# Attention and two expert layers on one core: VectorE, ScalarE and POOL put in a fixed order, as a pipeline in half steps

## The chip, the core and the metric

The kernel runs on one core of a Trainium2 chip. The metric is the time of one execution in microseconds (us). The core's engines are TensorE (PE in the rows; PEld is its weight load), VectorE (DVE), ScalarE (ACT), GpSimd (POOL) and SyncE (SP), which issues nearly all DMAs. TensorE's clock has two levels, 1.2 and 2.4 GHz; "granted clock" is the share of full speed.

## The reference

```python
kv  = einsum('bhsd,bhse->bhde', k, v)        # 4 batches, 8 heads, 576 rows, 64 wide
o   = einsum('bhsd,bhde->bhse', q, kv)
x   = o / rms(o) * g_norm                     # 2304 tokens x 512
h   = x @ w_in                                # 512 -> 2048, float64 weights
x   = where(h > 0, h, exp(min(h, 0)) - 1) @ w_out
for e in range(4):                            # w1[e]: 512 -> 1024, w2[e]: 1024 -> 512
    out += p[:, e:e+1] * (maximum(x @ w1[e], 0) @ w2[e])
```

## The kernel before

Every operand of a product is held as two parts, a rounded high part (ScalarE's copy) and the low remainder (a subtraction on POOL or VectorE, `split`), and a product is three matmuls: high x high, high x low, low x high. Tokens are worked on in 6 blocks j of 384.

*Attention and group zero* come from a table of places (`at_place`) and are emitted in that order with dependences that pin all four compute engines. *Layer one* then runs the other 14 columns c of 128 of the hidden layer in groups 1 to 4 (2, 4, 4 and 4 columns), each over all 6 blocks: a step (g, j, c) is `product1` (12 matmuls into a bank of 384 columns, two banks in turn), the ELU (`begin_elu`: two ScalarE operations; `end_elu`: one VectorE operation, line 465, which is the last to read the bank), `split_h`, and two steps later `emit_mm2` (12 matmuls). At a group's last column four accumulations (`into_acc`, line 483) go to VectorE. Beside this, `convert` turns the float64 rows of the next group's weights into float32 (five VectorE operations each, lines 151 to 179, two on ScalarE, then a split), 8 rows per group. `make_w` makes *forms*: layer two multiplies 2 x 2 blocks of each expert's weights with seven products P1 to P7 instead of eight, so that for each of 16 *quarters* (expert, w1 or w2, half) 7 combinations are made (4 subtractions on VectorE, line 232; a copy on ScalarE; a low part on POOL, or for two of the seven on VectorE once group four runs, line 241), stored to DRAM (`keptw`) and loaded again as `ws` when needed. `make_forms` makes the same combinations of the activations, once per pair of token blocks.

*Layer two* has 12 moves (3 pairs of token blocks x 4 experts). A move has 14 units of the first product (q, banks qa and qb) and, one move later, 14 of the second (m, banks ma and mb), which alternate. A unit is 12 matmuls, with its weights streamed four units ahead from DRAM by SP. P2 and P6 accumulate into the bank of P1 and P5, after ScalarE has copied that product out (lines 576, 655).

Behind the table of places nothing pins an engine's order: `emit_mm1`, `emit_mm2`, one step of `make_w` and so on are emitted one after another, and Tile's scheduler sets each engine's order by its own model of time:

```python
    for hh in range(2 * (len(steps) + LAG)):
        s, second = divmod(hh, 2)
        if not second and s < len(steps):
            emit_mm1(*steps[s][1:], nc.vector if s >= len(steps) - 3 else nc.gpsimd)
        if second and s >= LAG:
            emit_mm2(*steps[s - LAG])
        for op, *args in todo.get(hh, ()):
            op(*args)
```

## Time and profile before

| | us |
|---|---|
| median of 3 runs (lowest to highest) | 1253.01 (1250.71 to 1257.75) |
| the profiled execution | 1254.61 |
| its span in the trace | 1252.82 |
| PE, DVE, ACT, POOL busy | 1191.7, 794.6, 590.4, 664.2 |
| mean granted clock of TensorE | 0.977 |

The span goes from the first to the last instruction in the trace; the 1.8 us beside it lie outside. Busy times are shares of the whole span and mix stages with different limits. "Idle before" in a row is the engine's idle time just before the instruction, with what ended it.

### The profile page before, as it was taken

What the parts mean: (1) busy time and instruction counts of PE and PEld (TensorE: products, weight loads), DVE (VectorE), ACT (ScalarE), POOL (GpSimd) and SP (SyncE); (2) the same over time, 40 slices, a digit from 0 to 9 for tenths busy, and PEclk for the clock granted to TensorE, in tenths of its full rate; (3) what the DMA queues carried; (4) which work ended last, traced back from release to release, by engine and by line L of the source; (5) the groups of instructions that cost most, each with busy time, mean ns of one, the idle gap of its engine ahead of it and who ended that gap; (6) DMA issues with size and microseconds to landing.
All of it is one profiled execution on the core that took longest, in us unless ns stands there. A gap on an engine that the chain in (4) does not pass through costs nothing.

```text
span 1252.8 us, 18931 instructions
## 1 busy us (share of the span) xinstructions
PE 1191.7 (95%) x7039; PEld 1170.3 (93%) x7039; DVE 794.6 (63%) x950; ACT 590.4 (47%) x937; POOL 664.2 (53%) x521
## 2 busy tenths in 40 slices
PE   8899988897998999899999989999999899999997
PEld 8799978897998999899999989999999899999996
DVE  5878898969766456453546773546468545555475
ACT  3677665655555555443333434343345334333432
POOL 1124487688576568534455664445457634555533
PEclk9999988998998999999999999999999899999999
DMA  9943268666988765887887868878787688788883
GB/s 338 346 157 118 85 212 327 234 252 225 281 296 291 286 235 205 289 277 252 265 258 264 253 220 255 284 260 265 251 267 251 214 259 288 251 270 254 260 248 127
DMA packets 103455, 312.22 MB, mean 249 GB/s; under 512 B 19068, under 2 KB 23748, under 8 KB 101828
## 3 DMA queue, kind: packets, MB, share of 16 engines
q1 hardware_dynamic: 98532, 306.30, 73.2%
q10 hardware_dynamic: 4832, 4.72, 1.1%
q8 instruction: 56, 0.92, 0.3%
q14 instruction: 35, 0.29, 0.1%
HBM read 238.06 MB, written 72.91 MB: 248 GB/s over the span
## 4 chain that ended last, share of the span: by engine, by line
PE 52%; DVE 17%; DMA 8%; issue 5%; POOL 3%; ACT 2%; SPq 1%; POOLq 0%; DVEq 0%; ACTq 0%
PE ps_qb L552 15%; PE ps_mb L552 12%; PE ps_ma L552 11%; PE ps_qa L552 10%; DMA keptw<-wform 4%; DMA wraw<-in_moe_w_dram 3%; DVE wform L232 3%; POOL wform L241 1%; DVE acc L483 1%; DVE m L154 1%; DVE m L650 1%; DVE s L301 1%; DVE e L465 1%; DVE x L176 1%; DVE acc L651 1%
## 5 line engine op out<-in xcount | busy, mean ns | idle before, releaser
L193 POOL TENSOR_TENSOR h<-h 128x384 fp32r<-128x384 f32 x232 | 272.8, 1198 | 293.8 <-ACT h L183 292.4
L552 PE MATMUL ps_qb<-f,ws 128*128 128x384 f32 x1152 | 219.7, 338 | 9.1 <-DVE u L579 8.0
L183 ACT CAST h<-h 128x768 fp32r<-128x768 f32 x168 | 140.0, 835 | 164.7 <-PE ps_mb L552 83.1
L552 PEld LDWEIGHTS ps_qb<-f,ws 128*128 128x128 f32 x1152 | 203.6, 190 | 10.1 <-DVE u L579 8.6
L552 PE MATMUL ps_mb<-h,ws 128*128 128x384 f32 x1032 | 190.9, 335 | 0.7 <-ACT p L655 0.7
L552 PE MATMUL ps_ma<-h,ws 128*128 128x384 f32 x984 | 183.1, 334 | 2.0 <-ACT o L700 1.7
L552 PEld LDWEIGHTS ps_mb<-h,ws 128*128 128x128 f32 x1032 | 180.8, 189 | 1.3 <-ACT p L655 1.0
L552 PEld LDWEIGHTS ps_ma<-h,ws 128*128 128x128 f32 x984 | 171.5, 188 | 2.9 <-ACT o L700 1.9
L193 POOL TENSOR_TENSOR h<-e,h 128x384 fp32r<-128x384 f32 x91 | 107.1, 1179 | 114.5 <-ACT h L183 100.1
L552 PE MATMUL ps_qa<-f,ws 128*128 128x384 f32 x864 | 164.6, 335 | 1.3 <-DVE acc L483 1.3
L451 PE MATMUL ps_h<-x,w 128*128 128x384 f32 x384 | 135.6, 353 | 22.9 <-DVE e L465 22.9
L552 PEld LDWEIGHTS ps_qa<-f,ws 128*128 128x128 f32 x864 | 150.7, 188 | 1.8 <-DVE acc L483 1.8
L490 PE MATMUL ps_y<-h,w 128*128 128x384 f32 x384 | 131.7, 343 | 2.7 <-POOL h L193 2.7
L452 PE MATMUL ps_h<-x,w 128*128 128x384 f32 x384 | 132.6, 345 | 0.4 <-DVE x L427 0.4
L453 PE MATMUL ps_h<-x,w 128*128 128x384 f32 x384 | 132.6, 345 | 0.0
L491 PE MATMUL ps_y<-h,w 128*128 128x384 f32 x384 | 131.4, 342 | 0.1
L489 PE MATMUL ps_y<-h,w 128*128 128x384 f32 x384 | 117.9, 342 | 8.4 <-DVE acc L483 5.7
L572 ACT ACTIVATE h<-h 128x768 f32<-128x768 f32 x72 | 60.8, 847 | 119.6 <-DVE h L584 70.6
L451 PEld LDWEIGHTS ps_h<-x,w 128*128 128x128 f32 x384 | 75.3, 196 | 28.8 <-DVE e L465 28.6
L241 POOL TENSOR_TENSOR wform<-wform 128x512 fp32r<-128x512 f32 x54 | 77.0, 1430 | 31.9 <-ACT wform L239 11.8
L489 PEld LDWEIGHTS ps_y<-h,w 128*128 128x128 f32 x384 | 72.0, 191 | 11.8 <-DVE acc L483 7.8
L193 DVE TENSOR_TENSOR h<-h 128x768 fp32r<-128x768 f32 x52 | 50.5, 972 | 49.6 <-ACT h L183 49.6
(115 smaller groups left out, 1833.3 us busy)
## 6 DMA issues: line engine op xcount, KB each, us to landing
ws<-keptw SPq DMA_DIRECT2D x336, 512.0 KB, 4.4
keptw<-wform SPq DMA_DIRECT2D x112, 512.0 KB, 3.7
wraw<-in_moe_w_dram SPq DMA_DIRECT2D x32, 512.0 KB, 6.8
keptx<-x SPq DMA_DIRECT2D x6, 1536.0 KB, 6.0
x<-keptx SPq DMA_DIRECT2D x6, 1536.0 KB, 8.3
raw<-in_moe_w_in_dram SPq DMA_DIRECT2D x16, 512.0 KB, 4.4
raw<-in_moe_w_out_dram SPq DMA_DIRECT2D x16, 512.0 KB, 4.2
qkv<-in_k_dram SPq DMA_DIRECT2D x18, 256.0 KB, 5.4
```

The costliest lines, as they stand in the source:

```text
L183: nc.scalar.copy(hi, src)
L193: eng.tensor_tensor(out=l, in0=x, in1=h, op=ALU.subtract)
L232: nc.vector.tensor_tensor(out=f[:, 1], in0=minus[0], in1=minus[1], op=ALU.subtract)
L241: eng.tensor_tensor(out=f[:, 1].bitcast(F32R), in0=src, in1=f[:, 0], op=ALU.subtract)
L451: nc.tensor.matmul(ps, ah, bh, start=(kk == 0), stop=False)
L452: nc.tensor.matmul(ps, ah, bl, start=False, stop=False)
L453: nc.tensor.matmul(ps, al, bh, start=False, stop=(kk == KD - 1))
L489: nc.tensor.matmul(ps, bh[:, cols], hi, start=first, stop=False)
L490: nc.tensor.matmul(ps, bh[:, cols], lo, start=False, stop=False)
L491: nc.tensor.matmul(ps, bl[:, cols], hi, start=False, stop=last)
L552: nc.tensor.matmul(ps[:, c, :T], a, x[:, b, kk, :], start=start and kk == 0 and n == 0, stop=stop and kk == 1 and n == 2, skip_group_check ...
L572: nc.scalar.activation(into, src, AF.Relu)
```

## The change

Three things. First, behind the table of places VectorE, ScalarE and POOL now execute in the order in which the program emits (`in_program_order` at the end); TensorE and SP are still left to the scheduler. Second, the program emits in half steps (12 matmuls each). What follows from an operation on another engine is not emitted with it but put into a queue for a later half step (`after(n, ...)`, done by `tick`): an ELU's split comes one half step after its ending, a conversion's five operations are spread over five half steps, a form's low part comes one half step after its copy and its store another one later. In layer two a product is read out of its bank at the start of the next unit, ahead of all else. Third, the forms have tables of offsets: in layer one 12 of the 16 quarters are made, from group two on, 6 at 16 half steps each and 6 at 7; the last four are made in layer two's first pass over the experts, at 28 half steps each. A quarter's weights are loaded in four blocks of 256 KB ahead of time into six buffers, instead of two DMAs into one buffer. Before, the program's text also left some of the forms to layer two, but the scheduler did not: in the trace the first of the 64 subtractions on line 232 starts at 166.8 us and the last at 526.0 us, where layer two begins.

```diff
+    def after(n, op, *args):
+        queue.setdefault(clock[0] + n, []).append((op, args))
+
+    def tick(*starts):
+        for op, args in queue.pop(clock[0], []):
+            op(*args)
+        for op, *args in starts:
+            op(*args)
+        clock[0] += 1
...
+    def load_block(n, name):
...
+        b = blocks[n, name] = next_in("b", [P, 2, HK], "wraw")
+        row = (e * NC2 + half * NH + 2 * s) * P
+        nc.sync.dma_start(
+            out=b, in_=(w1, w2)[ab][row:row + 2 * P, cols * HK:(cols + 1) * HK].rearrange("(c p) f -> p c f", p=P)
+        )
...
+        def finish(name, of):
+            f = t[of] if of in t else next_in("f", [P, 2, 2, HK], "wform")
+            src = f[:, 1] if of in t else blocks[n, of]
             nc.scalar.copy(f[:, 0].bitcast(F32R), src)
+            after(1, finish_low, name, f, src)
+
+        def finish_low(name, f, src):
             eng = nc.vector if name in late["on_vector"] else nc.gpsimd
             eng.tensor_tensor(out=f[:, 1].bitcast(F32R), in0=src, in1=f[:, 0], op=ALU.subtract)
...
+            after(1, keep, name, f)
...
+    FORMS_SLOW = "t1:0 t2:2 P5:3 t3:4 t4:6 P3:7 b12:8 b11:8 P4:9 P7:10 b22:10 P1:11 P2:13 b21:14 P6:15", 16
+    FORMS_FAST = "t1:0 t2:1 P5:2 t3:2 b12:3 b11:3 b22:3 t4:3 P3:4 P4:4 P7:5 P1:5 P2:6 P6:7 b21:8", 7
+    FORMS_LATE = "t1:0 t2:4 P5:5 t4:8 P3:9 t3:12 P7:13 b12:14 P4:16 P1:18 P2:20 P6:22 b11:22 b22:25 b21:25", 28
...
         form("A11", a11, nc.gpsimd)
+        yield
         form("S2", s2, other)
         yield
         form("A12", a12, nc.gpsimd)
+        s4 = sums(a12, s2, ALU.subtract, s2)
+        yield
         form("S1", s1, other)
-        s4 = sums(a12, s2, ALU.subtract, s2)
+        yield
+        form("S4", s4, nc.gpsimd)
         s3 = sums(a11, a21, ALU.subtract, s1)
...
-    begins = 2 * (len(steps) - NB * NF)
...
-            for hh in range(begins, begins + length, every):
-                at_step(hh, make_one, converting)
-            at_step(begins + length - 1, finish_all, converting)
+            for n, row in enumerate(pieces):
+                at_step(begins + n * (3 if g == 1 else 6), convert, len(rows))
+                rows.append(row)
...
-            emit_mm1(*steps[s][1:], nc.vector if s >= len(steps) - 3 else nc.gpsimd)
-        if second and s >= LAG:
-            emit_mm2(*steps[s - LAG])
-        for op, *args in todo.get(hh, ()):
-            op(*args)
...
+        if not second:
+            if s < len(steps):
+                product1(*steps[s][1:])
+            while pending:
+                into_acc(*pending.pop(0))
+            if 0 < s <= len(steps):
+                split_h(*steps[s - 1][1:], nc.vector if s >= len(steps) - 2 else nc.gpsimd)
+            tick(*todo.get(hh, ()))
+        else:
+            if s >= LAG:
+                emit_mm2(*steps[s - LAG])
+            if s < len(steps):
+                begin_elu(*steps[s][1:])
+            tick(*todo.get(hh, ()))
+            if s < len(steps):
+                end_elu(*steps[s][1:])
...
+    for n in range(IN_LAYER1, len(quarters)):
+        at = plan_forms(n, at, FORMS_LATE, lambda half, step: starts.setdefault(half, []).append(step))
...
+            for kind in "qm":
+                if evict:
+                    evict()
+                evict = None
+                if kind == "q" and n < len(moves):
+                    stream(u + AHEAD)
+                    evict = emit_q(u, moves[n], *Q_UNITS[k])
+                    u += 1
...
+                tick(*starts.pop(clock[0], ()))
...
+    in_program_order(start_order, E_.DVE, E_.Activation, E_.Pool)
```

How the change moves instructions, at three places. The first is VectorE early in group two of layer one, before:

```order
L232 TENSOR_TENSOR wform<-wraw 128x512
L232 TENSOR_TENSOR wform<-wraw,wform 128x512 x2
L465 SCALAR_TENSOR_TENSOR e<-e,ps_h 128x384
L151 TENSOR_SCALAR x<-raw 128x512
L154 TENSOR_SCALAR m<-raw 128x512
L168 SCALAR_TENSOR_TENSOR m<-raw,m 128x512
L154 TENSOR_SCALAR m<-raw 128x512
L168 SCALAR_TENSOR_TENSOR m<-raw,m 128x512
L176 SCALAR_TENSOR_TENSOR x<-raw,x 128x512
L465 SCALAR_TENSOR_TENSOR e<-e,ps_h 128x384
```

and VectorE early in the same group now (lines 495, 507 and 261 are what 465, 483 and 232 were; 936 to 959 are four of the conversion's five operations):

```order
L495 SCALAR_TENSOR_TENSOR e<-e,ps_h 128x384
L507 TENSOR_TENSOR acc<-ps_y,acc 128x384 x4
L168 SCALAR_TENSOR_TENSOR m<-raw,m 128x512
L953 SCALAR_TENSOR_TENSOR x<-raw,x 128x512
L261 TENSOR_TENSOR wform<-wraw 128x512
L959 SCALAR_TENSOR_TENSOR m<-m,x 128x512
L495 SCALAR_TENSOR_TENSOR e<-e,ps_h 128x384
L261 TENSOR_TENSOR wform<-wraw,wform 128x512
L495 SCALAR_TENSOR_TENSOR e<-e,ps_h 128x384
L936 TENSOR_SCALAR x<-raw 128x512
```

Before, six conversion operations stood between two ELU endings, in runs that the scheduler chose. Now at most four operations stand there (two conversion operations and a subtraction among them).

The second is VectorE at the end of the first pair of token blocks in layer two, between the reading of the pair's last product (line 594, now 620) and that of the next pair's second one (579, now 604). Before:

```order
L594 TENSOR_TENSOR h<-ps_qb,u 128x768
L675 TENSOR_TENSOR c<-ps_ma,u 128x768
L650 TENSOR_TENSOR m<-c,p 128x768
L651 TENSOR_TENSOR acc<-acc,m 128x768
L599 TENSOR_TENSOR h<-h 128x768
L600 TENSOR_TENSOR h<-h 128x768
L601 TENSOR_TENSOR h<-h 128x768
L193 TENSOR_TENSOR h<-h 128x768
L579 TENSOR_TENSOR u<-ps_qb,p 128x768
```

and now:

```order
L620 TENSOR_TENSOR h<-ps_qb,u 128x768
L685 TENSOR_TENSOR acc<-acc,m 128x768
L327 TENSOR_TENSOR s<-acc 128x768
L713 TENSOR_TENSOR c<-ps_ma,u 128x768
L628 TENSOR_TENSOR h<-h 128x768
L684 TENSOR_TENSOR m<-c,p 128x768
L629 TENSOR_TENSOR h<-h 128x768
L685 TENSOR_TENSOR acc<-acc,m 128x768
L191 TENSOR_TENSOR f<-s,f 128x768
L604 TENSOR_TENSOR u<-ps_qb,p 128x768
```

Between the two readings stood seven operations; now there are eight, among them a sum and a low part of the new pair's forms (lines 327 and 191).

The third is SP, where layer two begins (`ws` is a weight tile that is loaded, `keptw` a form that is stored). Before, the last stores and then 40 loads in a row:

```order
L530 DMA ws<-keptw 128x1024
L247 DMA keptw<-wform 128x1024 x2
L530 DMA ws<-keptw 128x1024 x2
L247 DMA keptw<-wform 128x1024
L530 DMA ws<-keptw 128x1024 x40
L618 DMA p<-p_dram 128x768
L530 DMA ws<-keptw 128x1024 x27
```

and now, some way into the first pass:

```order
L555 DMA ws<-keptw 128x1024 x8
L276 DMA keptw<-wform 128x1024
L555 DMA ws<-keptw 128x1024 x5
L276 DMA keptw<-wform 128x1024
L555 DMA ws<-keptw 128x1024
L248 DMA wraw<-in_moe_w_dram 128x2x256
L555 DMA ws<-keptw 128x1024 x2
L276 DMA keptw<-wform 128x1024
L555 DMA ws<-keptw 128x1024 x2
```

Stores that wait for POOL or VectorE, and loads of blocks, now stand among the weight tiles through the whole first pass.

## Rows read from the trace of the kernel before

**Rows 1.** The page, parts 1 and 2: busy time, and clock in 40 slices.

```profile
PE 1191.7 (95%) x7039; PEld 1170.3 (93%) x7039; DVE 794.6 (63%) x950; ACT 590.4 (47%) x937; POOL 664.2 (53%) x521
...
PEclk9999988998998999999999999999999899999999
```

**Rows 2.** Waits of TensorE: who, for whom: us in total, times, longest.

```profile
PE ps_h L451 <- DVE e L465: 22.9, 14, 4.9
PE ps_qb L552 <- DVE u L579: 8.0, 2, 4.0
...
PE ps_y L489 <- ACT h L183: 1.9, 1, 1.9
...
PE ps_mb L552 <- ACT p L655: 0.7, 1, 0.7
```

**Rows 3.** Timeline of PE in group two: start us, us, instruction.

```profile
198.49 0.33 PE L451 MATMUL ps_h<-x,w 128*128 128x384 f32 x1
...
200.57 0.33 PE L489 MATMUL ps_y<-h,w 128*128 128x384 f32 x1
```

**Rows 4.** Stretches: us, busy of PE, PEld, DVE, ACT, POOL, clock, DMA share, GB/s.

```profile
106.60:159.60 53.00, 52.24 (x299) 51.36 (x298) 46.14 (x74) 36.00 (x70) 26.70 (x21) 1.00 0.31 93
159.60:285.30 125.70, 109.42 (x569) 106.33 (x569) 108.08 (x129) 74.60 (x143) 95.14 (x71) 0.92 0.71 258
285.30:408.60 123.30, 110.92 (x587) 106.84 (x586) 89.36 (x110) 66.34 (x131) 84.24 (x64) 0.93 0.83 275
408.60:510.00 101.40, 99.52 (x572) 98.66 (x571) 57.73 (x77) 54.47 (x105) 66.97 (x55) 1.00 0.70 246
```

**Rows 5.** The same view: around the end of TensorE's longest wait.

```profile
208.90:215.70 6.80, 4.65 (x15) 4.65 (x16) 5.03 (x7) 3.86 (x7) 4.56 (x4) 0.50 0.96 351
```

**Rows 6.** Timeline of VectorE in group two, the same columns as rows 3.

```profile
169.87 0.54 DVE L465 SCALAR_TENSOR_TENSOR e<-e,ps_h 128x384 f32<-128x384 f32 x1
...
171.29 1.76 DVE L232 TENSOR_TENSOR wform<-wraw,wform 128x512 f32<-128x512 f32 x1
172.98 0.68 DVE L168 SCALAR_TENSOR_TENSOR m<-raw,m 128x512 f32<-128x512 uint32 x1
...
178.10 0.54 DVE L465 SCALAR_TENSOR_TENSOR e<-e,ps_h 128x384 f32<-128x384 f32 x1
```

**Rows 7.** Groups by line, VectorE, group three: count | busy us, mean ns | idle before.

```profile
L232 DVE TENSOR_TENSOR wform<-wraw 128x512 f32<-128x512 f32 x12 | 14.7, 1227 | 10.9 <-DMA wraw<-in_moe_w_dram 9.1 <-issue 1.9
...
L232 DVE TENSOR_TENSOR wform<-wraw,wform 128x512 f32<-128x512 f32 x12 | 13.6, 1131 | 1.5 <-DMA wraw<-in_moe_w_dram 1.4
```

**Rows 8.** The page, part 6: DMA issues, KB each, us to landing.

```profile
ws<-keptw SPq DMA_DIRECT2D x336, 512.0 KB, 4.4
keptw<-wform SPq DMA_DIRECT2D x112, 512.0 KB, 3.7
wraw<-in_moe_w_dram SPq DMA_DIRECT2D x32, 512.0 KB, 6.8
...
x<-keptx SPq DMA_DIRECT2D x6, 1536.0 KB, 8.3
```

**Rows 9.** The same view as rows 4: the highest rates of transfer.

```profile
0.00:40.00 40.00, 36.00 (x409) 32.67 (x410) 23.90 (x51) 17.28 (x29) 3.51 (x11) 1.00 0.97 350
330.00:335.00 5.00, 5.00 (x30) 4.85 (x30) 4.47 (x5) 1.82 (x4) 3.96 (x3) 1.00 1.00 398
```

**Rows 10.** The same view, layer two: a steady stretch, two ends of pairs.

```profile
560.00:720.00 160.00, 160.00 (x925) 160.00 (x925) 90.67 (x88) 65.24 (x81) 82.68 (x66) 1.00 0.81 258
720.00:760.00 40.00, 36.00 (x200) 35.65 (x200) 26.31 (x22) 16.41 (x21) 28.57 (x21) 0.96 0.68 226
960.00:1000.00 40.00, 36.00 (x197) 35.65 (x197) 27.51 (x24) 15.06 (x19) 28.09 (x20) 0.91 0.65 219
```

**Rows 11.** Timeline of VectorE at the first end of a pair.

```profile
727.53 0.94 DVE L594 TENSOR_TENSOR h<-ps_qb,u 128x768 f32<-128x768 f32 x1
...
739.62 0.94 DVE L579 TENSOR_TENSOR u<-ps_qb,p 128x768 f32<-128x768 f32 x1
```

More of the change, by code (lines that the diff above doesn't have):

```diff
@@ L193, in split @@
             eng.tensor_tensor(out=l, in0=x, in1=h, op=ALU.subtract)
+    def split(hi, lo, src, eng):
+        nc.scalar.copy(hi, src)
+        split_lo(lo, src, hi, eng)
+    queue = {}
+    clock = [0]
+    def after(n, op, *args):
[6 more added lines that the diff above has]
+        clock[0] += 1
     wf = {}
@@ L212, in attention_moe_kernel @@
     kept_w = {}
[L214 to L238 removed]
+    IN_LAYER1 = 12
@@ new lines, in attention_moe_kernel, with next_in @@
+    quarters = [(ab, e, s) for e in range(E) for ab in (0, 1) for s in (0, 1)]
+    blocks = {}
+    rings = {"b": 0, "f": 0}
+    def next_in(ring, shape, name):
+        of = late[ring]
+        pool, tag = of[rings[ring] % len(of)]
+        rings[ring] += 1
+        return pool.tile(shape, F32, tag=tag, name=name)
+    def load_block(n, name):
+        if n >= len(quarters):
+            return
+        ab, e, s = quarters[n]
+        half, cols = (int(name[2]) - 1, int(name[1]) - 1) if ab == 0 else (int(name[1]) - 1, int(name[2]) - 1)
+        b = blocks[n, name] = next_in("b", [P, 2, HK], "wraw")
[3 more added lines that the diff above has]
+        )
@@ L239, in finish, with make_w, sum_ @@
+    def make_w(n):
+        ab, e, s = quarters[n]
+        t = {}
+        def sum_(name, a, b):
+            f = t[name] = next_in("f", [P, 2, 2, HK], "wform")
+            a, b = (t[x][:, 1] if x in t else blocks[n, x] for x in (a, b))
+            nc.vector.tensor_tensor(out=f[:, 1], in0=a, in1=b, op=ALU.subtract)
+        def finish(name, of):
+            f = t[of] if of in t else next_in("f", [P, 2, 2, HK], "wform")
+            src = f[:, 1] if of in t else blocks[n, of]
             nc.scalar.copy(f[:, 0].bitcast(F32R), src)
+            after(1, finish_low, name, f, src)
+        def finish_low(name, f, src):
@@ L323, in make_forms @@
         form("A22", a22, nc.gpsimd)
+        yield
     at = ExitStack()
@@ L752, in plan_norm, with in_program_order @@
             at_place(x, emit_x, t)
+    before = {}
+    E_ = mybir.EngineType
+    def in_program_order(begin, *engines):
+        for i in nc.cur_bb.bb.instructions[begin:]:
+            if i.engine not in engines:
+                continue
+            if i.engine in before:
+                tc.add_manual_dep(
+                    i, before[i.engine].name,
+                    mybir.DependencyInfo(mybir.DependencyClass.NoSync, mybir.DependencyReason.DATA),
+                    reason="order",
+                )
+            before[i.engine] = i
     def busy(n):
@@ L937, in attention_moe_kernel @@
         at_step(begins + hh, make_one, of_p)
-    of_forms = [begins + n for n in (22, 25, 28, 32, 36)]
-    for hh in of_forms:
-        at_step(hh, make_one, forms_of_0)
-    for hh in range(25, 2 * len(steps) - 4):
-        if hh == begins:
-            at_step(hh, lambda: late.update(on_vector=("P2", "P7")))
-        if hh not in of_forms and (hh % 2 or hh > begins):
-            at_step(hh, make_one, making)
-        if hh > begins and hh % 4 == 2:
-            at_step(hh, make_one, making)
+    for hh in (21, 25, 26, 33, 34, 41, 42, 50):
+        at_step(begins + hh, make_one, forms_of_0)
+    at = begins - 2 * NB * NF * 2 + 4
+    for n in range(IN_LAYER1):
+        at = plan_forms(n, at, FORMS_SLOW if n < 6 else FORMS_FAST, lambda hh, step: at_step(hh, *step))
+    at_step(begins + 7, lambda: late.update(
+        on_vector=("P2", "P7"), f=[late["f"][0], (wl_p, "w")] * 3 + [late["f"][0]]
+    ))
     LAG = 2
@@ L951, in attention_moe_kernel @@
         s, second = divmod(hh, 2)
-        if not second and s < len(steps):
-            emit_mm1(*steps[s][1:], nc.vector if s >= len(steps) - 3 else nc.gpsimd)
-        if second and s >= LAG:
-            emit_mm2(*steps[s - LAG])
-        for op, *args in todo.get(hh, ()):
-            op(*args)
-    for _ in forms_of_0:
-        pass
+        if not second:
[14 more added lines that the diff above has]
+                end_elu(*steps[s][1:])
+    while pending:
+        into_acc(*pending.pop(0))
+    while queue:
+        tick()
     layer1.close()
-    late["wf"] = with_wm.enter_context(tc.tile_pool(name="wf2", bufs=3, reuse_waits="tile"))
+    rings["b"] = 0
+    late["b"] = late["b"][:1]
+    late["f"] = [(with_wm.enter_context(tc.tile_pool(name="wf2", bufs=3, reuse_waits="tile")), "f")]
     late["psum"] = ctx.enter_context(tc.tile_pool(name="psum2", bufs=1, space=bass.MemoryType.PSUM, reuse_waits="tile"))
```

324 lines of the change are left out of this document (151 added, 173 removed).

## The prediction

> **What bounds the kernel now.** I read five views in this order: the page's shares, TensorE's waits, the busy time by stretch, the timelines of VectorE where TensorE waits, and the transfers. TensorE is busy for 95% of the span and its granted clock falls below full in only a few slices [rows 1]. So the work outside TensorE matters only where TensorE stops, and there is little to win anywhere else. Its waits name VectorE: 22.9 us before a product of layer one, 14 times, until VectorE has read the PSUM bank (line 465), and 8.0 us in two waits of 4.0 us in layer two (line 579) [rows 2].
>
> The stretches show where this lies. A step of layer one is 24 matmuls; a run of 12 takes 200.57 - 198.49 = 2.08 us [rows 3], so a step needs 4.16 us and 24 steps 99.8 us. Group two of the layer (24 steps) took 125.7 us, group three 123.3 us, group four 101.4 us, group one (12 steps, 49.9 us needed) 53.0 us [rows 4]. Groups two and three therefore lose 25.9 and 23.5 us. Of group two's loss 125.7 - 109.4 = 16.3 us is idle time, and the other 9.6 us are matmuls at the lower clock: the mean there is 0.92, and around the end of the longest wait, 4.9 us [rows 2], 6.8 us are granted at 0.50, the lower of the two levels, 1.2 GHz [rows 5]. A wait removed also gives back the slow stretch behind it.
>
> Why VectorE is late: in group two it has 108.1 us of work [rows 4] for 99.8 us of matmuls. Between two readings of a product's bank (169.87 and 178.10) stand six operations on SBUF tiles, and operations of one size take 0.68 us in one place and 1.76 us in another [rows 6]. In group three it is busy for only 89.4 us, but it also stands still for 9.1 us until a weight block has landed [rows 7], and everything behind that operation stands with it. The reason for both is the order that the scheduler chose: form work of the second layer is pulled forward, so that groups two and three carry 5 and 6 quarters of it (20 and 24 subtractions on line 232, the latter in two rows of 12 [rows 7]), at the same time as the conversions.
>
> **The change, group by group.** Groups two and three now hold 3 quarters each, one conversion per six half steps, and blocks loaded about eight half steps (16 us) ahead. Group two's VectorE then issues 8 x 5 conversion operations, 12 subtractions, 24 ELU endings and 24 accumulations: 100 operations. At the mean of the 129 in its row, 108.08 / 129 = 0.838 us, that is 83.8 us for 99.8 us of matmuls. Group three: 100 x 89.36 / 110 = 81.2 us. What loss is left? Group one has 46.1 us of VectorE work for 49.9 us (92%) and loses 3.1 us, so 6 per 100; group four has 58% and loses 1.6 us [rows 4]. These are the ends for a well-ordered queue; 84% and 81% lie nearer to the first, so I take 105 us for each group. **Group two -20.7, group three -18.3.** Wrong order could leave all of it (0 instead of -39), and no loss at all would be -49.4. Group one keeps its load (8 x 5 + 12 + 24 = 76 operations, now 74): 0.
>
> Group four takes 6 quarters, as many as group three had, at 7 half steps (14.6 us) each. VectorE: 24 subtractions, 12 low parts, 48 endings and accumulations, 4 sums and 2 more low parts, 90 x 57.73 / 77 = 67.5 us; POOL: 22 + 30 + 14 = 66 operations x 66.97 / 55 = 80.4 us [rows 4]. Neither fills 99.8 us. The transfers come closer. A quarter writes 7 x 0.524 MB and reads 1.05 MB, 4.72 MB; six of them less the last reads, two x tiles (1.57 MB) and four weight tiles are 32.5 MB [rows 8], nearly all in 87.4 us: 372 GB/s. The stretches show 350 GB/s at a share of 0.97 for 40 us and 398 at 1.00 for 5 us [rows 9], and group three 275 at 0.83, so 331 at a full share [rows 4]. At 398 it fits, at 350 / 0.97 = 361 it ends 2.6 us late, at 331 10.8 us. Also, a block that is loaded late stops the in-order queue, as in [rows 7]. I take **+4** (ends -1.5 and +11).
>
> Layer two. A full stretch holds 925 matmuls in 160 us, 231 in 40; the two stretches of 40 us at the ends of pairs hold 200 and 197 [rows 10], so 31 + 34 are missing, 65 x 40 / 231 = 11.3 us in all, waits and slow clock together. The cause is VectorE's queue: the reading of the last product's bank starts at 727.53, that of the next one only at 739.62, behind seven operations [rows 11]. The new order does not empty this place. Eight operations still stand between the two readings (the order above), and the first such place also gets the last quarter's forms; but the sums and low parts on both sides are one per two half steps, and POOL's slices no longer come in one burst. Half of it goes: **-6** (ends 0 and -11.3).
>
> New in layer two are the four quarters. In its first 14 units (29.1 us) SP issues 14 weight tiles, 7 stores and 6 blocks, 12.6 MB or 433 GB/s; the three following moves (58.2 us each) carry 28 + 7 tiles, 1.05 MB of blocks and the probabilities, 19.8 MB or 340 GB/s, where the steady stretch has 258 [rows 8, 10]. At 361 GB/s the first move ends 5.8 us late and the others on time; the first three or four tiles are read before it begins, which covers 4 us or more. Stores also wait on SP for POOL with weight tiles queued behind them; four tiles of lead (8.3 us) cover this. I take **+4** (ends 0 and, at 331 GB/s, +13.8). VectorE, ScalarE and POOL have the room: 90.7, 65.2 and 82.7 us of 160 in the steady stretch [rows 10].
>
> The 331 to 398 GB/s above are measured here. The Trainium skill (DMA: Bandwidth & Descriptors, Specifications) gives about 358 GB/s as a core's limit to HBM and so speaks against asking for 372 and 433. By that figure group four ends 3.4 us late and the first move 6.1 us, 9.5 instead of my 8, and the sum would be 1.5 us higher; the 398 GB/s of [rows 9] do not support a hard limit there.
>
> **Sum:** -20.7 - 18.3 + 4 - 6 + 4 = -37.0. The profiled execution took 1254.61 us (span 1252.82), so 1217.6. It lies 1.6 us above the median of the three runs, 1253.01, so I forecast **1216 us**.
>
> **Rivals.** *Everything fits* (nothing is lost): groups two to four give 25.9 + 23.5 + 1.6, the pair ends 11.3: -62.3, so 1191. For it: TensorE runs for 160.00 of 160 us at full clock when nothing is late [rows 10]. Against it: VectorE above 80% with operations of 0.68 to 1.78 us.
>
> *Transfers become the bound* in group four and layer two's first pass: at 331 GB/s 10.8 + 13.8 = 24.6 instead of 8, so 1233; at 258 / 0.81 = 319 GB/s still more of the gain goes. For it: 433 and 372 GB/s asked. Against it: the 398 GB/s seen.
>
> *Slower: ScalarE's fixed order delays evictions in layer two.* In every one of 12 moves four products accumulate into a bank that a ScalarE copy must first read, with a single other unit (2.08 us) between. Now TensorE waits once for such a copy (0.7 us), and once for 1.9 us on another ScalarE operation [rows 2], for the scheduler lets ScalarE take what it expects to be ready. If a fixed order put a waiting operation ahead of these copies, 48 x 1.3 us (the middle of the two) = 62 us would come back: 1278. It decides the sign from 37 / 48 = 0.77 us per copy on. Against it: the copy is emitted first in its half step.
>
> *The order changes little*: SP's and TensorE's queues are still the scheduler's, and if the waits come from those, the time stays at 1253.
>
> **Numbers.** The forecast with its terms' ends (1200 to 1232) 0.57, everything fits 0.12, transfers 0.17, slower 0.08, no change 0.06. The range 1191 to 1242 leaves out the last two and a little of the ends, some 0.19. A measurement of this kernel tells about 0.5% (6.3 us) from no change: faster 0.86, within 0.06, slower 0.08.
>
> **What would show it.** Right: groups two and three at 100 to 107 us each with VectorE below 90 us; TensorE's wait on the ELU ending under 8 us instead of 22.9; hardly a slice with the clock at 0.9; first subtractions of the forms evenly 33 us apart, then 14.6. Group four's transfers at a share above 0.9 would show the asked rate, and 103 to 109 us there my +4. The first 30 us of layer two should show TensorE waits on weight tiles of a few us. Wrong: groups two and three above 110 us; waits on ScalarE's copies in layer two that repeat every move; or pair ends without any wait.

## The result, and the profile after

The changed kernel takes **1218.59 us** (median of 4 runs, 1216.34 to 1219.27) against 1252.94 us: a ratio of 0.9718, 95% interval 0.9686 to 0.9749. The forecast was 1216. The profiled execution has a span of 1216.1 us, 36.7 less than before.

The page of the kernel after, parts 1 and 2, against [rows 1]:

```profile
PE 1175.8 (97%) x7039; PEld 1157.4 (95%) x7039; DVE 795.5 (65%) x951; ACT 587.1 (48%) x937; POOL 659.5 (54%) x520
...
PEclk9999999999999999999999989999999999999999
```

The engines execute as many instructions as before. TensorE has the same 7039 matmuls and is busy for 16 us less, since more of them run at the full clock: the mean granted clock is 0.991 instead of 0.977, and one slice lies below 9 instead of five. TensorE's waits in the kernel after (lines 495, 604 and 692 are what 465, 579 and 655 were), against [rows 2]:

```profile
PE ps_qb L576 <- DVE u L604: 9.5, 3, 5.2
PE ps_h L481 <- DVE e L495: 7.6, 9, 2.2
...
PE ps_qa L576 <- DMA ws<-keptw: 1.0, 2, 0.7
...
PE ps_mb L576 <- ACT p L692: 0.7, 1, 0.7
```

The wait on the ELU ending fell from 22.9 to 7.6 us, the waits at the ends of pairs rose from 8.0 to 8.8 (5.2 and 3.65; the third of the 9.5 us, 0.7, lies in layer two's first move), the weight tiles cost 1.0 (in moves 5 and 9) and ScalarE's copies 0.7. The stretches of the kernel after, columns as in [rows 4]: groups two and three, group four with the passage to layer two, layer two's first four moves, the first move after a pair's end, and the time around the end of the wait there:

```profile
162.70:263.70 101.00, 100.19 (x577) 99.87 (x577) 70.96 (x108) 63.16 (x121) 61.91 (x51) 1.00 0.59 198
263.70:363.60 99.90, 99.90 (x579) 99.90 (x578) 70.52 (x100) 61.44 (x118) 66.69 (x54) 1.00 0.70 228
363.60:479.40 115.80, 107.83 (x603) 103.55 (x601) 74.42 (x100) 64.34 (x127) 91.42 (x72) 1.00 0.86 307
...
479.40:513.20 33.80, 32.02 (x181) 31.20 (x182) 14.89 (x17) 13.39 (x20) 12.01 (x9) 1.00 0.92 316
513.20:569.30 56.10, 56.10 (x325) 56.10 (x324) 38.15 (x34) 27.21 (x38) 39.20 (x30) 1.00 0.97 350
569.30:627.60 58.30, 58.30 (x339) 58.30 (x338) 41.05 (x37) 25.91 (x36) 39.22 (x29) 1.00 0.95 343
627.60:685.80 58.20, 58.20 (x337) 58.20 (x336) 47.12 (x41) 26.82 (x37) 45.91 (x31) 1.00 0.95 328
685.80:753.40 67.60, 62.41 (x350) 62.02 (x349) 44.27 (x38) 26.95 (x34) 41.43 (x32) 0.95 0.73 250
...
700.40:707.30 6.90, 5.74 (x18) 5.74 (x19) 6.83 (x7) 1.00 (x2) 4.52 (x3) 0.51 0.43 166
```

In group three TensorE stands still for nothing (99.90 of 99.90). Moves 1 to 3 run without a gap too, at a transfer share of 0.95 to 0.97. VectorE in group two, where [rows 6] had six operations between two endings:

```profile
177.38 0.54 DVE L495 SCALAR_TENSOR_TENSOR e<-e,ps_h 128x384 f32<-128x384 f32 x1
177.84 0.42 DVE L936 TENSOR_SCALAR x<-raw 128x512 uint32<-128x512 uint32 x1
178.18 0.68 DVE L261 TENSOR_TENSOR wform<-wraw,wform 128x512 f32<-128x512 f32 x1
178.78 1.24 DVE L943 TENSOR_SCALAR m<-raw 128x512 uint32<-128x512 uint32 x1
179.94 0.54 DVE L495 SCALAR_TENSOR_TENSOR e<-e,ps_h 128x384 f32<-128x384 f32 x1
```

Here three operations stand between two endings and the next ending comes 2.6 us later, not 8.2. That is one of the short places. The longest in group two is now 6.7 us, with eight operations (four accumulations and four others), where it was 8.4; the "at most four operations" given with the change are those beside the accumulations, and three of the four in the order shown there are conversions. Where the time came from, by stage, with the kernels of the experiments beside it. A stage is counted from the first matmul of its first product to that of the next stage; the last two columns are moves 4 to 7, and from move 8 to the end of the span; times with * are single ones:

| kernel | group 1 | 2 | 3 | 4 + passage | moves 0-3 | 4-7 | 8 to end | time |
|---|---|---|---|---|---|---|---|---|
| before | 53.0 | 125.7 | 123.3 | 111.6 | 207.6 | 241.6 | 283.5 | 1252.94 |
| after | 56.3 | 101.0 | 99.9 | 115.8 | 206.4 | 244.7 | 285.7 | 1218.59 |
| e1_unpinned | 53.6 | 122.6 | 112.7 | 109.0 | 208.6 | 242.1 | 284.4 | 1241.72 |
| e2_vector_pinned | 51.5 | 101.4 | 101.5 | 124.0 | 228.7 | 241.1 | 280.4 | 1238.88* |
| e11_vector_only | 52.2 | 100.6 | 104.2 | 115.1 | 206.3 | 244.7 | 285.0 | 1218.52* |
| e5_dense | 56.5 | 123.7 | 137.6 | 106.2 | 206.4 | 243.2 | 286.3 | 1269.08* |
| e3_four_blocks | 56.4 | 101.0 | 99.8 | 154.4 | 206.4 | 244.3 | 285.9 | 1258.08* |
| e7_g4_no_store | 56.4 | 101.1 | 99.8 | 111.4 | 206.4 | 244.1 | 285.9 | 1215.70* |
| e8_seven_five | 56.5 | 102.3 | 99.8 | 111.7 | 206.5 | 243.8 | 286.4 | 1214.56* |
| e6_no_late | 56.4 | 101.1 | 99.8 | 114.7 | 205.3 | 241.9 | 285.9 | 1213.67* |
| e4_seam_defer | 52.3 | 101.0 | 99.8 | 115.8 | 206.4 | 236.7 | 279.6 | 1201.06* |
| e9_seam_defer_75 | 52.3 | 101.6 | 99.8 | 110.8 | 206.5 | 236.8 | 280.0 | 1198.04 |
| e10_seam_defer_74 | 52.3 | 102.2 | 99.8 | 107.1 | 212.9 | 240.4 | 279.5 | 1204.58 |
| e12_seam_defer_84 | 52.3 | 102.4 | 108.1 | 105.9 | 206.4 | 237.0 | 280.0 | 1202.26 |

Groups two and three gave 48.1 us; group one lost 3.3, group four 4.2 and layer two 4.1.

### The profile page after: what moved, and what is told of

Read it like the earlier page. It is cut to its first block, busy times and chain, and to the rows that moved or that the text cites. A ratio compares the mean times of both kernels' runs of the same rounds, so it can differ in the third digit from the quotient of the medians.

```text
span 1216.1 us, 18927 instructions
## 1 busy us (share of the span) xinstructions
PE 1175.8 (97%) x7039; PEld 1157.4 (95%) x7039; DVE 795.5 (65%) x951; ACT 587.1 (48%) x937; POOL 659.5 (54%) x520
## 4 chain that ended last, share of the span: by engine, by line
PE 52%; DVE 4%; issue 1%; POOL 1%; DMA 1%; ACT 1%; ACTq 0%; DVEq 0%; POOLq 0%
PE ps_qb L576 15%; PE ps_ma L576 14%; PE ps_mb L576 11%; PE ps_qa L576 10%; DMA ws<-keptw 1%; DVE acc L685 1%; DVE m L684 1%; DVE f L191 1%; PE ps_mb L731 0%; POOL c L707 0%; DVE h L191 0%; POOL h L191 0%; DVE h L629 0%; DVE h L628 0%; DVE u L604 0%
## 5 line engine op out<-in xcount | busy, mean ns | idle before, releaser
L191 POOL TENSOR_TENSOR h<-h 128x384 fp32r<-128x384 f32 x232 | 280.2, 1232 | 212.4 <-ACT h L638 206.1
L576 PEld LDWEIGHTS ps_qb<-f,ws 128*128 128x128 f32 x1152 | 202.7, 190 | 11.9 <-DVE u L604 10.5
L576 PE MATMUL ps_ma<-h,ws 128*128 128x384 f32 x1080 | 200.0, 335 | 0.8 <-DVE h L191 0.7
L191 POOL TENSOR_TENSOR h<-e,h 128x384 fp32r<-128x384 f32 x91 | 102.9, 1131 | 172.0 <-ACT h L194 160.1
L576 PEld LDWEIGHTS ps_ma<-h,ws 128*128 128x128 f32 x1080 | 187.9, 188 | 1.8 <-DVE h L191 1.0
L576 PE MATMUL ps_mb<-h,ws 128*128 128x384 f32 x936 | 174.3, 337 | 1.6 <-ACT o L738 0.8
L638 ACT CAST h<-h 128x768 fp32r<-128x768 f32 x168 | 139.9, 833 | 72.3 <-PE ps_ma L576 37.2
L576 PEld LDWEIGHTS ps_mb<-h,ws 128*128 128x128 f32 x936 | 165.1, 190 | 2.2 <-issue 1.1
L481 PE MATMUL ps_h<-x,w 128*128 128x384 f32 x384 | 130.5, 340 | 7.6 <-DVE e L495 7.6
L514 PE MATMUL ps_y<-h,w 128*128 128x384 f32 x384 | 128.8, 335 | 1.7 <-POOL h L191 1.7
L482 PE MATMUL ps_h<-x,w 128*128 128x384 f32 x384 | 128.9, 336 | 0.4 <-DVE x L457 0.4
L483 PE MATMUL ps_h<-x,w 128*128 128x384 f32 x384 | 129.0, 336 | 0.0
L515 PE MATMUL ps_y<-h,w 128*128 128x384 f32 x384 | 128.6, 335 | 0.1
L513 PE MATMUL ps_y<-h,w 128*128 128x384 f32 x384 | 119.3, 339 | 1.9 <-ACT h L194 1.2
L495 DVE SCALAR_TENSOR_TENSOR e<-e,ps_h 128x384 f32<-128x384 f32 x96 | 52.7, 549 | 81.4 <-ACT e L491 69.8
L194 ACT CAST h<-e 128x384 fp32r<-128x384 f32 x96 | 49.0, 511 | 73.3 <-DVE e L495 73.2
```

The lines of the kernel that those rows point to most:

```text
L191: eng.tensor_tensor(out=l, in0=x, in1=h, op=ALU.subtract)
L481: nc.tensor.matmul(ps, ah, bh, start=(kk == 0), stop=False)
L482: nc.tensor.matmul(ps, ah, bl, start=False, stop=False)
L483: nc.tensor.matmul(ps, al, bh, start=False, stop=(kk == KD - 1))
L495: nc.vector.scalar_tensor_tensor(out=e, in0=e, scalar=-1.0, in1=ps_h.pop((j, c)), op0=ALU.add, op1=ALU.max)
L513: nc.tensor.matmul(ps, bh[:, cols], hi, start=first, stop=False)
```

## The experiments

### What emptied groups two and three

**e1_unpinned.** The last line of the change goes:

```diff
-    in_program_order(start_order, E_.DVE, E_.Activation, E_.Pool)
```

> The changed kernel without its last line, the pin of VectorE, ScalarE and POOL behind the table of places; the emission in half steps, the spread of the forms and the six block buffers stay. Theory (the pinned order is what removes the waits): the scheduler again builds runs of slow operations between two ELU endings, groups two and three take 110 to 125 us each instead of 101.0 and 99.9, and the whole 1235 to 1255 us. Rival (the spread of work over the half steps and the early loads do it, the pin only confirms it): groups two and three stay within 3 us of 101.0 and 99.9, and the whole is 1213 to 1225 us.

Measured: 1241.72 us, 0.9912 of before (0.988 to 0.9943), groups two and three 122.6 and 112.7. The theory held: left free, VectorE executes 22 form subtractions in group two, where the emission has 12. But work pulled forward is not all of it. Group three of this kernel has only 10 subtractions, two fewer than the emission, its VectorE is far from full, and 12.9 us are still lost there (its stretch, columns as before, and TensorE's wait in it):

```profile
282.00:395.90 113.90, 104.43 (x584) 102.73 (x585) 66.05 (x90) 55.52 (x110) 60.40 (x47) 0.99 0.53 164
```

```profile
PE ps_h L481 <- DVE e L495: 9.3, 5, 4.2
```

Ahead of the longest of these waits six conversion and form operations, 8.6 us of work, stand between two ELU endings (282.62 and 291.31 us). So the order costs by its runs, too, and not only by what it pulls forward.

**e2_vector_pinned.** The kernel before, VectorE alone pinned in that program's own emission order:

```diff
+    for i in nc.cur_bb.bb.instructions[second_part:]:
+        if i.engine is not mybir.EngineType.DVE:
+            continue
...
```

> The kernel before with VectorE alone pinned behind the table of places, in the order in which that program's text has it (conversions, forms and endings emitted together, block loads late as before). If any fixed order helps because it keeps form work out of groups two and three, they fall from 125.7 and 123.3 us to 100 to 106. If the pipeline (what follows on another engine comes a half step later) is what counts, a pin alone makes VectorE wait for ScalarE and for loads with the ELU endings queued behind it: groups two and three stay at 120 or become longer than before, and the whole is 1250 to 1350 us.

Measured: 101.4 and 101.5 us, all but 2 us of the gain in these two groups, without the pipeline, the early loads or the new buffers; the first of the two expectations held there. The old text, too, puts 3 quarters into each. Stretches of this kernel, columns as before (groups two, three, and 139 us from group four on):

```profile
158.80:261.30 102.50, 101.70 (x584) 100.84 (x584) 71.59 (x107) 63.57 (x122) 68.50 (x54) 1.00 0.59 212
261.30:362.80 101.50, 100.67 (x577) 99.68 (x576) 68.40 (x100) 61.20 (x118) 66.76 (x54) 1.00 0.64 208
362.80:502.00 139.20, 123.99 (x679) 119.15 (x678) 80.20 (x108) 70.75 (x136) 93.11 (x75) 0.98 0.82 296
```

What the rest of the change is good for shows behind them: group four and the passage take 124.0 us (111.6 before) and the first four moves 228.7 (207.6). In group four VectorE's pinned queue stands on blocks that are loaded late, and two waits of TensorE, 2.7 and 5.2 us, follow on two of these; what the first four moves lose was not taken apart. VectorE's waits in group four of this kernel (us in total, times, longest):

```profile
DVE wform L232 <- DMA wraw<-in_moe_w_dram: 16.6, 3, 8.2
```

**e11_vector_only.** The changed kernel with `in_program_order(start_order, E_.DVE)`.

> The changed kernel with only VectorE pinned behind the table of places; ScalarE and POOL are left to the scheduler. Theory (it is VectorE's order that keeps the forms in their groups; the other two follow from it): groups two and three within 2 us of 101.0 and 99.8, group one shorter by 2 to 4 us since ScalarE's order at the seam is free again, the whole 1208 to 1220 us. Rival (ScalarE and POOL must be fixed too): groups two to four lose 5 us or more, the whole 1222 or above. The sign of my fourth rival (a fixed ScalarE order costs in layer two) is seen too: if freeing ScalarE shortens the moves between the ends of pairs, 58.2 us each now, it cost something.

Measured: 1218.52 us. Group one is 4.1 us shorter, group three 4.3 longer, the rest alike. The theory held for the sum, not for group three, which lies outside its 2 us. In this single run, pinning ScalarE and POOL gives in one place what it takes in another. Moves between ends of pairs last 58.2 us with and without it, so a fixed ScalarE order delays no eviction there.

**e5_dense.** The order still pinned, but 11 quarters in groups two and three, as many as before had there:

```diff
-        at = plan_forms(n, at, FORMS_SLOW if n < 6 else FORMS_FAST, ...
+        at = plan_forms(n, at, FORMS_DENSE if n < 11 else FORMS_FAST, ...
+    FORMS_DENSE = FORMS_FAST[0], 8
```

> The changed kernel with as much form work in groups two and three as before had there: 11 quarters, one per eight half steps (44 subtractions instead of 24), one quarter left in group four; the order still pinned. Theory (the order is the gain, the amount of work is not): groups two and three 100 to 105 us each though VectorE is busy 85 to 95 us in them, group four about 100, the whole 1205 to 1222. Rival (the gain is that 5 of 11 quarters left these groups): groups two and three 112 to 125 us each, as before, and the whole 1235 to 1255.

Measured: 123.7 and 137.6 us, 1269.08 in all. My theory fell. The rival's direction held, and the loss is more than it said (112 to 125 us each, 1255 at most): a fixed order that leaves the work there gains nothing. But it isn't the sum of the work either. Stretches of this kernel, groups two and three:

```profile
162.90:286.80 123.90, 107.40 (x582) 101.54 (x581) 86.41 (x120) 69.41 (x134) 88.49 (x68) 0.99 0.76 262
286.80:422.00 135.20, 109.33 (x559) 104.44 (x560) 80.42 (x110) 71.00 (x138) 95.34 (x74) 0.91 0.81 272
```

No engine is full. Timelines of ScalarE, SP and VectorE in the same kernel (start us, us, instruction, idle before and what ended it):

```profile
190.57 0.62 ACT L266 CAST wform<-wraw 128x512 fp32r<-128x512 f32 x1 [3.43 <-DMA keptw<-wform]
...
193.08 0.62 ACT L266 CAST wform<-wraw 128x512 fp32r<-128x512 f32 x1 [0.96 <-DMA keptw<-wform]
193.60 0.48 ACT L491 ACTIVATE e<-ps_h 128x384 f32<-128x384 f32 x1
```

```profile
187.89 7.60 SPq L276 DMA_DIRECT2D keptw<-wform  x4
195.55 0.46 SPq L248 DMA_DIRECT2D wraw<-in_moe_w_dram  x1
```

```profile
194.75 0.56 DVE L496 SCALAR_TENSOR_TENSOR e<-e,ps_h 128x384 f32<-128x384 f32 x1 [7.46 <-ACT e L492]
```

A form's copy on ScalarE needs one of four form buffers, and gets it when an earlier form's store has landed. The stores stand on SP until POOL has made the low part, and the block loads stand behind the stores. The ELU stands behind the copy, so VectorE waits 7.46 us for it. Over both groups ScalarE's form copies wait for stores, and SP's stores for POOL, thus:

```profile
ACT wform L266 <- DMA keptw<-wform: 27.6, 13, 5.6
```

```profile
SPq L276 <- POOL wform L271: 124.0, 69, 8.0
```

In groups two and three of the kernel after, ScalarE's copies never wait for a store.

**e12_seam_defer_84.** With the two edits of e4 below, 8 quarters in groups two and three (one per 12 half steps) and 4 in group four (one per 11).

> The changed kernel with the seam and the deferred scalings, and 8 quarters over groups two and three (one per 12 half steps), 4 in group four (one per 11), 4 in layer two as in the change. It is a point between 7 quarters in groups two and three, which cost 1 us (201.4 for both groups against 200.8 with 6), and 11, which cost 60. If the chain from VectorE over ScalarE and POOL to SP's stores has a limit that 11 quarters are beyond and 8 are not: groups two and three 200 to 206 us together, group four with the passage 107 as with 4 quarters before, the first four moves 206 to 207, the whole 1193 to 1198 us. If the loss grows evenly with each quarter over 6 (12 us for each): 222 to 228 us together and the whole 1212 or more.

Measured: 1202.26 us, 0.9577 of before (0.9555 to 0.9599). Groups two and three together take 210.5 us: 200.8 with 6 quarters, 201.4 with 7 (e9), 261.3 with 11. It is neither an even rise nor a free eighth quarter: most of the 9 us is one stall. VectorE in group three of this kernel:

```profile
298.73 1.31 DVE L261 TENSOR_TENSOR wform<-wraw 128x512 f32<-128x512 f32 x1
307.57 0.69 DVE L261 TENSOR_TENSOR wform<-wraw,wform 128x512 f32<-128x512 f32 x1 [7.53 <-DMA keptw<-wform]
308.18 0.55 DVE L496 SCALAR_TENSOR_TENSOR e<-e,ps_h 128x384 f32<-128x384 f32 x1
```

and the 10 us ahead of it and the 12 around it:

```profile
290.00:300.00 10.00, 10.00 (x60) 10.00 (x59) 9.97 (x11) 6.45 (x13) 10.00 (x8) 1.00 0.86 329
300.00:312.00 12.00, 8.04 (x38) 7.72 (x37) 4.47 (x9) 4.48 (x9) 6.05 (x5) 0.79 0.87 308
```

POOL had no gap from 290 to 300, so a low part and its store came late, the buffer too, and the ELU ending stood behind the subtraction that needed it. TensorE has 38 matmuls in these 12 us, where the rate of the row above makes 72: 34 are missing, 5.7 us, of which 4.0 are idle time and the rest the lower clock. That more buffers would mend it was not tried.

The runs together say what the order and the amount of form work are worth in groups two and three. With 44 subtractions in them, they take 249.0 us in a free order (before) and 261.3 in a fixed one (e5); with 32, 235.3 free (e1, 22 + 10) and 210.5 fixed (e12, 16 + 16); with 24, 200.8 fixed. A fixed order is worth 25 us at the same amount of work, and nothing at all when the amount is too large for it.

### What group four needs

**e3_four_blocks.** Four buffers for weight blocks instead of six, blocks loaded later:

```diff
-    FORMS_FAST = "... b12:3 b11:3 b22:3 t4:3 ... P6:7 b21:8", 7
+    FORMS_FAST = "... b12:3 t4:3 ... b11:6 P2:6 b21:7 P6:7 b22:8", 7
...
-                      [(layer1.enter_context(tc.tile_pool(name="wm2", ...
```

> The changed kernel with four buffers for weight blocks instead of six (as much memory as before had), so that the blocks of the next quarter are loaded two to four half steps ahead at most instead of eight. Theory (the order is the gain; the transfers in groups two and three run at 0.6 to 0.7 of their time): groups two and three within 2 us of 101.0 and 99.9; group four, at 14.6 us for a quarter, 1 to 5 us longer; the whole 1219 to 1226. Rival (early loads are what keeps VectorE from standing still, as in the 9.1 us wait of before): groups two and three 105 to 112 us each, VectorE's wait on weight blocks there 5 us or more, the whole 1230 or above.

Measured: groups two and three unchanged, as the theory said, and not as the rival; but group four takes 154.4 us, 38.6 more where I had allowed 1 to 5, and the whole 1258.08: all of the change's gain is gone. VectorE's waits in group four of this kernel:

```profile
DVE wform L261 <- DMA wraw<-in_moe_w_dram: 49.8, 10, 10.2
```

With 14.6 us for a quarter, ten late blocks stop VectorE for 5 us each, and with it the ELU endings behind it: stalls like those of [rows 7].

**e7_g4_no_store.** The stores of quarters 6 to 11 are left out, and layer two multiplies with quarters 0 to 5 in their place:

```diff
         def keep(name, f):
+            if NO_STORE <= n < IN_LAYER1:
...
+                kept_w[ab, e, s, name] = kept_w[ab_, e_, s_, name]
+                return
```

> The changed kernel with the 42 stores of the six quarters of group four left out (layer two reads quarters 0 to 5 in their place); loads, VectorE, ScalarE and POOL keep their work. If the 4 us that group four and the passage to layer two lost (111.6 us before, 115.8 now) come from the transfers, or from the queue of SP in which block loads stand behind stores that wait for POOL: that stretch falls to 104 to 108 us and the whole to 1206 to 1211. If POOL's own work (91.4 us busy) is the bound: it stays at 113 or more and the whole at 1215 or more.

Measured: 111.4 us for the stretch, between the two. The stores account for 4.4 us: VectorE's and ScalarE's waits for them, 10.7 and 3.3 us there in the kernel after, fall to 0.7 and nothing. The transfer share falls from 0.86 to 0.39, and yet 7 us remain over the 104 that the stretch's 24 + 26 runs of 12 matmuls need (the stretch, and TensorE's wait in it):

```profile
366.20:477.60 111.40, 107.09 (x603) 105.38 (x601) 74.94 (x100) 64.47 (x127) 90.54 (x71) 0.98 0.39 129
```

```profile
PE ps_h L486 <- DVE e L500: 3.7, 3, 2.0
```

What these 7 us hang on is not shown. TensorE waits for three ELU endings, and from 440 us to the end of the stretch POOL has no gap (37.60 of 37.60 us) while VectorE's subtractions beside it take up to 1.78 us instead of 0.68; but no run lightens POOL alone.

**e8_seven_five.** 7 quarters at 13 half steps in groups two and three, 5 at 9 in group four.

> The changed kernel with the twelve quarters of layer one spread as 7 at 13 half steps over groups two and three and 5 at 9 half steps in group four, instead of 6 at 16 and 6 at 7. If the amount of form work in a group sets what it loses, and a group with half a quarter more than three still has room (VectorE 71 and POOL 62 to 67 us of 100): groups two and three 100 to 103 us each, group four with the passage 108 to 112 instead of 115.8, the whole 1211 to 1217. If groups two and three are at the edge (five and a half quarters each took 125 to 130 us): 104 to 110 us each, and the whole 1220 to 1232.

Measured: 102.3, 99.8 and 111.7 us, 1214.56: there is room for the seventh. (The "125 to 130 us" of the expectation are 123.7 and 137.6 in the table.)

**e10_seam_defer_74.** With the two edits of e4, 7 quarters in groups two and three, 4 in group four, 5 in layer two at 22 half steps each.

> As e9_seam_defer_75, but with 7 quarters in groups two and three, 4 in group four at 11 half steps each, and 5 in layer two's first pass at 22 half steps each. If POOL and SP's queue are what group four still loses by, it falls from 111.7 us (5 quarters) to 106 to 109, the first four moves stay at 206 to 207, and the whole is 1194 to 1197 us. If a quarter is no longer hidden in layer two when it comes every 22 half steps, the first four moves or the first end of a pair give 2 to 6 us back and the whole is 1198 to 1203.

Measured: 1204.58 us, 0.96 of before (0.9575 to 0.9625). Group four falls to 107.1 as the theory said, but the rival's cost came true and outweighs it, with 9.9 us more than the 2 to 6 it said: the first move 37.9 us instead of 33.8, the fourth 60.6 instead of 58.2, the first move behind the pair's end 63.5 instead of 60.1. In the first move TensorE waits for ScalarE:

```profile
PE ps_qa L577 <- ACT h L608: 2.5, 1, 2.5
```

### What the four late quarters cost

**e6_no_late.** Expert 3 multiplies with the forms of expert 0; its own are neither loaded nor made.

```diff
-        at = plan_forms(n, at, FORMS_LATE, ...
+        for q in Q_ORDER:
+            kept_w[ab, e, s, q] = kept_w[ab, 0, s, q]
```

> The changed kernel without the four quarters of forms in layer two's first pass: expert 3 multiplies with the forms of expert 0, so its blocks are not loaded and its forms not made. Theory (the four quarters are hidden, as the stretch of the first four moves says: 207.6 us before, 206.4 now): the first four moves 205 to 207 us, the wait at the first end of a pair a little shorter, the whole 1214 to 1218 us. Rival (the term of the prediction, 4 us, is there but another saving hides it): the first four moves 202 us or less and the whole 1210 to 1213.

Measured: moves 0 to 3 take 205.3 us, 1.1 less, and the first move after the pair's end 65.0 instead of 67.6. So the quarters cost about 1 us in their moves and 2.6 behind them, by single runs (the kernels that differ only in layer one take 66.6 to 67.6 us for that move). VectorE and POOL make the last quarter's low parts only around that end, in the kernel after:

```profile
681.74 0.76 DVE L271 TENSOR_TENSOR wform<-wraw,wform 128x512 fp32r<-128x512 f32 x1
```

```profile
689.34 2.05 POOL L271 TENSOR_TENSOR wform<-wraw,wform 128x512 fp32r<-128x512 f32 x1
```

### The seam and the ends of pairs

**e4_seam_defer.** ScalarE's chain of order is cut behind the table of places; at the ends of the first two pairs three scaling operations (P4's addition into the output, P7's product with the probabilities and its addition; lines 684 and 685) come ten half steps later:

```diff
     in_program_order(begin, E_.PE, E_.DVE, E_.Activation, E_.Pool)
+    before.pop(E_.Activation)
...
-            after(1 if last else 2, into_out, step, c, 1, 1)
+            ahead = e == E - 2 and p < NPAIR - 1
+            after(1 if last else 2, into_out, step, c, 1, 1, 10 if ahead else 1)
...
-            after(1, into_out, step, c, 1, 0)
+            after(10 if e == E - 2 and p < NPAIR - 1 else 1, into_out, step, c, 1, 0)
```

> The changed kernel with two edits in places far apart. At the seam behind the table of places ScalarE's fixed order is cut once, so that the first ELU of the pipeline need not stand behind group zero's last accumulation copies: theory, group one falls from 56.3 to 53 to 54 us; rival (the order at the seam is not the cause), it stays at 56 or more. At the ends of the first two pairs in layer two, two scalings' additions into the output (line 685) and one more come ten half steps later, so that five instead of eight VectorE operations stand before the reading of bank qb (line 604): theory (VectorE's queue), the two waits of 5.2 and 3.65 us fall below 2 and 1.5 us, some 4 to 8 us less with the slow stretches behind them; rival (POOL, busy from 676 to 705 us without a gap, or the ScalarE copies behind it), the waits stay at 3 us or more. The whole: 1206 to 1212 us by both theories, 1217 to 1220 by both rivals.

Measured: 1201.06 us, 17.5 less than the change and more than both theories said. At the seam, the kernel after has on TensorE, at the end of group one's first product, and on ScalarE:

```profile
108.33 0.33 PE L483 MATMUL ps_h<-x,w 128*128 128x384 f32 x1
```

```profile
113.02 0.62 ACT L194 CAST w<-m 128x512 fp32r<-128x512 f32 x1 [1.52 <-DVE m L179]
114.21 1.00 ACT L505 COPY acc<-ps_y 128x384 f32<-128x384 f32 x2 [0.57 <-PE ps_y L515]
116.61 1.00 ACT L505 COPY acc<-ps_y 128x384 f32<-128x384 f32 x2 [1.40 <-PE ps_y L515]
117.51 0.50 ACT L490 ACTIVATE e<-ps_h 128x384 f32<-128x384 f32 x1
```

ScalarE waits for products of TensorE while the ELU of group one's first product, which is done at 108.7, stands behind: it starts at 117.51, 8.8 us later. With the chain cut it starts 2.8 us after its product is done (112.53 and 109.8), and group one takes 52.3 us; e11, where ScalarE has no pin at all, has 52.2. VectorE at the first end of a pair, in the kernel after, which answers to [rows 11]:

```profile
688.42 0.94 DVE L620 TENSOR_TENSOR h<-ps_qb,u 128x768 f32<-128x768 f32 x1
...
695.55 1.75 DVE L629 TENSOR_TENSOR h<-h 128x768 f32<-128x768 f32 x1
697.23 1.74 DVE L685 TENSOR_TENSOR acc<-acc,m 128x768 f32<-128x768 f32 x1
698.89 1.75 DVE L191 TENSOR_TENSOR f<-s,f 128x768 fp32r<-128x768 f32 x1
700.57 0.94 DVE L604 TENSOR_TENSOR u<-ps_qb,p 128x768 f32<-128x768 f32 x1
```

and with the three operations deferred:

```profile
685.57 0.95 DVE L620 TENSOR_TENSOR h<-ps_qb,u 128x768 f32<-128x768 f32 x1
...
692.83 0.96 DVE L604 TENSOR_TENSOR u<-ps_qb,p 128x768 f32<-128x768 f32 x1
```

7.26 us from one reading to the next instead of 12.15, and TensorE waits 0.3 us instead of 5.2. The moves behind the two ends fall from 67.6 and 65.0 to 60.1 and 59.5 us, 13.0 in all, for 8.5 us of waits: the rest is the clock, 0.51 for 6.9 us around the end of the first wait (above) and 0.50 for 3.4 us around that of the second. POOL is no less busy there, 44.7 of 60 us from 680 us on against 37.2 from 683 us on before the edit, so the rival falls.

**e9_seam_defer_75** joins e4 and e8.

> The changed kernel with the seam cut and the deferred scalings of e4_seam_defer and the 7 + 5 quarters of e8_seven_five. The stages are apart, so the gains should add: 1201.1 less some 3 us in group two to four (316.7 to 313.8 for the sum of the three stretches there): 1197 to 1200 us. If the two interfere, or e4's single time was a lucky one, 1201 or more.

Measured: **1198.04 us** (1195.73 to 1200.67), 0.9549 of before (0.9522 to 0.9576), faster than both kernels. By the stages in the table the gains add.

## Why the prediction was right, and where it wasn't

The time is 2.6 us from the forecast, and the direction and the main cause are shown: the order that the scheduler had given VectorE in groups two and three, by the forms that it pulled forward (e2, e5) and by its runs between two ELU endings (e1 against e12). But that the sum fits, -37.0 predicted and -36.7 in the spans, is luck in part. The terms missed by -9.1 (groups two and three), +3.3 (group one), +0.2 (group four), +11.3 (from move 4 on) and -5.2 (layer two's first pass), and these cancel.

- *Groups two and three, -20.7 and -18.3.* They gave 24.7 and 23.4. The mechanism was right, the size off in one step: 100 operations at the mean of [rows 4]'s 129, 0.838 us. Now 108 took 70.96 us, 0.657 each, so 71 of 100 us are filled, not 84, and the 5 us that I left in each group as a loss are not there (1.2 and 0.1). With fewer forms, fewer VectorE operations run beside POOL, and those cost less: the form subtractions 0.85 and 1.02 us in group two, where they cost 1.15 and 1.48. POOL is busy there for 61.9 of 101.0 us, before for 95.1 of 125.7; that they cost less for this reason is read from the traces, and no run tested it alone. A mean share of VectorE also says little of the wait: e1 loses 12.9 us in group three with VectorE busy for 66.05 of 113.9 us. I also gave the load ahead of time a part in this, and took the 9.1 us of [rows 7] for one standstill. They are several waits (with the 1.4 us of its second row five, 10.5 us, the longest 4.9), and e2 and e3 show that early loads have no part in these groups; e11 shows that ScalarE's and POOL's pins have none in group two.
- *Group one, 0.* It lost 3.3 us: I had not looked at the seam where the new chain is tied to the old one. e4 shows it.
- *Group four, +4.* It came out at +4.2 with the passage. The number is luck as far as the mechanism goes. Its transfers reached a share of 0.86 over the stretch, not 0.9, at 307 GB/s instead of 372, and the stretch takes 12 us more than its matmuls need. Of these, 4.4 us hang on the stores (e7), and the rest goes with the form work in the group: 111.7 us with five quarters (e8), 107.1 with four (e10). Whether it is POOL's or VectorE's part of that work stays open. I had dismissed POOL at 80 of 99.8 us; it is busy for 91.4 of 115.8, and from 440 to 456 us without a gap (16.00 of 16).
- *Ends of pairs, -6, "half of it goes".* Nothing went; it got worse, by 5.3 us from move 4 to the end. The moves behind the ends took 67.6 and 65.0 us (63.7 and 64.4 before). The queue had eight operations instead of seven and took as long, 12.15 us against 727.53 to 739.62 in [rows 11]; I had counted the eight and still argued from their even spacing. With three of them moved away the loss goes (e4).
- *Layer two's first pass, +4.* It gained 1.2. TensorE never waits for a weight tile in it, though the transfers are at 0.92 to 0.97, and the waits of a few us that I named as a sign did not come. The 433 GB/s were never asked: in the first 29.1 us SP issued 12 tiles, 6 stores and 2 blocks, not 14, 7 and 6, and 8.9 MB moved instead of 12.6 (305 GB/s). Four tiles of lead hold. Leaving the quarters out gives 1.1 us (e6).
- *Rivals.* ScalarE's fixed order: TensorE waits 0.7 us in all for one copy, and e11 takes nothing off the moves. Transfers as the bound: moves 1 to 3 ran at 328 to 350 GB/s with TensorE at 58.20 of 58.20 us. The Trainium skill's limit of about 358 GB/s for a core ("DMA: Bandwidth & Descriptors", Specifications) lies just above these rates; no run here shows TensorE held by it, and the 398 GB/s of [rows 9], over 5 us, lie above it. *The order changes little*: e1, with all three engines left to the scheduler, comes nearest to it, at 1241.72.

## What to carry to other kernels

A scheduler that fills idle time can pull optional work forward, to where the engine is needed next, and can build runs of it ahead of what TensorE waits for; pin the engine that TensorE waits for, and put the optional work where there is room. A fixed order makes every operation that waits hold up all behind it, so loads must be early and buffers free by then: here two block buffers fewer, with the later loads that they force, cost as much as the order gained. And count the queue between two readings of a bank: what is not needed soon can be moved out of it for nothing.

## What was not expected of the hardware

How much POOL costs VectorE, and how sharply it depends on where an operand lies. In the kernel after, the form subtractions with two SBUF operands (`wform<-wraw,wform`) take 0.68 to 0.69 us in all 9 cases with no POOL operation beside them and 0.85 to 1.51, 1.34 in the mean, in the 12 that lie wholly beside one; line 604, which reads PSUM, takes 0.94 to 0.96 in all 24 cases, 14 of them wholly beside POOL. The Trainium skill (SBUF — State Buffer, "Who interferes with whom") has the two engines take turns at a shared pair of ports; these durations agree. An order that thins out POOL's work between two readings of a bank should then shorten VectorE's too, which no run tested by itself. And a wait is dearer than its length: around the end of the 5.2 us above, 6.9 us are granted at 0.51.
